# A linear-attention block beside an MLP on one Trainium2 core: another order for loading and transposing x at the start

## The chip, the cores and the metric

The kernel runs on one core of a Trainium2 chip. The metric is device time in microseconds; the time before is 206.69 us, the median of three runs (206.48 to 206.86). The profiles are of one execution each. In them PE is TensorE's matmuls, PEld its weight loads, DVE is VectorE, ACT is ScalarE, POOL is GpSimd and SP is the queue of SyncE, which here issues nearly all DMAs. Times inside a profile are microseconds from the start of its span.

## What is computed

x is 2048 tokens by 640 features in bf16. It is normalized, and the output is x plus a linear attention and plus an MLP of the normalized x, both without any dependence between them:

```python
xn = _layernorm(x, axis=-1)
return x + _A_ref(xn, A_wqkv, A_wo) + _B_ref(xn, B_w1, B_b1, B_w2, B_b2)
```

The part that this document is about is the start: the normalization and the MLP's first layer.

```python
m = jnp.mean(x, axis=axis, keepdims=True)
v = jnp.var(x, axis=axis, keepdims=True)
return (x - m) / jnp.sqrt(v + eps)
...
h = jnp.einsum("bsd,df->bsf", x, w1) + b1
h = _gelu(h)
return jnp.einsum("bsf,fd->bsd", h, w2) + b2
```

W1 is 640 by 1536. The attention has 32 heads of 20 features and needs the projections by Wqkv, for which the same normalized and transposed x is used later.

## The kernel before

Tokens are handled in 16 tiles of 128 (x0 to x15 below), features in five blocks of 128 (k = 0 to 4), the hidden features of the MLP in twelve blocks of 128 (jb = 0 to 11).

**From x to a matmul.** A tile of x is loaded with its tokens on the partitions (dma_x, tile xPK). VectorE takes its statistics in two halves (ln_half, line 357) and joins them (ln_aggr, line 365); GpSimd adds the epsilon (line 360) and raises the variance to the power -1/2 (line 367); VectorE normalizes (ln_norm, line 381, tile xn_tm). For the first layer a tile must then be transposed, features on the partitions (tile xnT). There are two ways. TensorE can transpose five blocks of 128 into PSUM, from where ScalarE or VectorE copies them (tr_part and cp_part for tiles 0 and 1, lines 342, 350 and 351; transp and xnT_copy for tile 2, lines 389 and 397). Or a DMA transposes it from SBUF to SBUF (xnT_dma, line 263, issued by SP), as for tiles 3 to 15.

**The order of matmuls** is the list named plan, written by hand. Tiles 0 and 1 are worked block row by block row of W1 as these rows are loaded (hk, line 439: a token group, a number of tiles, jb, and the blocks k), with all twelve jb open in PSUM banks 0 to 5 at once. Line 439 takes 128 columns where one tile is worked, 256 where both are. Then come the units that have all five k at once: h_pack, line 423, one tile of 128 columns, four jb in one bank; h_unit, line 408, two or four tiles, 256 or 512 columns, one jb. After the last product ScalarE applies the activation and writes HG (lines 446, 428 and 412). Marks in the plan place other work: "T1" the transposes of tile 1 with the statistics of tiles 2 and 3, "TC" the last blocks of tile 0, "T2" the transpose of tile 2 and the normalization of tile 3 and, through ln_rest, all of tiles 4 to 15.

**What sets the order.** Each engine executes its instructions in the order in which the program calls for them, and each instruction waits for what it reads and for the buffers that it writes. So does SP: a DMA transpose that waits for a normalization holds back every DMA behind it. All loads and transposes of this start are issued by SP, except half of x0 and b1. Before, SP issues the loads of x0 to x11 and of W1's five row blocks first (lines 273 to 286), then the transposes of tiles 3 to 7, then the load of x12 to x15, then the transposes of tiles 8 to 15, and then the loads of Wqkv and of the later weights. PSUM banks of the units are taken in turn from a ring of eight (take); at(b) sets the ring to a bank.

The block after this start uses xnT with Wqkv (lines 564 and 570), then the attention's sums, then the output, with the MLP's second layer (line 771).

Of the kernel before, what the change touches and what calls it, by code (L numbers as in the profile page):

```python
# [112 lines left out]
def bass_parallel_sum__linear_attn_block__dense_activation_gelu__prompt_kernel(  # L113
# [27 lines left out]
    with contextlib.ExitStack() as es:  # L141
# [67 lines left out]
        def bank(b, lo=0, hi=512):  # L209
            return ps[:, b * 512 + lo: b * 512 + hi]  # L210
# [58 lines left out]
        def dma_w1(k):  # L269
            dma("sync", W1[:, k, :], w1v[:, k, :], [r_W1[k]])  # L270
# [3 lines left out]
            dma(("sync", s_)[i], x_in[:, 0, lo:hi], xv[0:P, lo:hi], [r_x[0][i]])  # L274
        dma_x(1, 1)
        dma_w1(0)
        dma_w1(1)
        dma_w1(2)
        dma_x(2, 1)
        dma_w1(3)  # L280
        dma_x(3, 1)
        dma_w1(4)
        dma_x(4, 2)
        dma_x(6, 2)
        dma_x(8, 2)
        dma_x(10, 2)

        Pl.ins(v, lambda e: e.memset(pm[0:P // 2], 1.0), writes=[r_pm])
        Pl.ins(v, lambda e: e.memset(pm[P // 2:P], -1.0), writes=[r_pm])
# [93 lines left out]
                    ALU.subtract, ALU.mult),  # L383
                    reads=r_x[t] + [r_aggr[s], r_rstd[t]], writes=[r])

        def transp(t):
            b = take(1)
            pT = bank(b).bitcast(BF16)[:, 0:D]
            Pl.ins(pe, [(lambda e, k=k: e.transpose(pT[:, k * P:(k + 1) * P],
                                                    xn_tm[:, t, k * P:(k + 1) * P], ident[:]))  # L390
                        for k in range(DT)],
                   reads=r_xn[t] + [r_ident], writes=[B_[b]])
            return b

        def xnT_copy(t, b):
            pT = bank(b).bitcast(BF16)[:, 0:D]
            Pl.ins(v, lambda e: e.tensor_copy(xnT[:, :, t * P:(t + 1) * P],
                                              pT.rearrange("p (k q) -> p k q", k=DT)),
                   reads=[B_[b]], writes=r_xnT[t])

        def xnT_dma(t):
            dma_t("sync", xnT[:, :, t * P:(t + 1) * P], xn_tm[:, t, :], r_xnT[t], reads=r_xn[t])

# [28 lines left out]
        def at(b):  # L432
            ring[0] = b
# [43 lines left out]
        k_list = lambda t, n, ks, lo=0, hi=JT: [(t, n, jb, ks) for jb in range(lo, hi)]  # L477
        pack = lambda t, lo, hi: [(t, jb) for jb in range(lo, hi, 4)]
        plan = k_list(0, 1, [0]) + ["T1"] + k_list(0, 1, [1]) + k_list(1, 1, [0]) + k_list(1, 1, [1]) + ["TC"]
        plan += k_list(0, 1, [2]) + k_list(1, 1, [2]) + k_list(0, 2, [3], 0, 8) + ["T2"]  # L480
        plan += k_list(0, 2, [4], 0, 8) + k_list(0, 2, [3, 4], 8)
        plan += pack(2, 0, 8) + h_list(2, 2, 8, JT) + pack(3, 0, 8) + h_list(4, 2, 0, 7) + h_list(6, 2, 0, 7)
        plan += h_list(4, 4, 7, JT) + h_list(8, 4, 0, JT) + h_list(12, 4, 0, JT)

        def ln_rest():
            def out(t):
                ln_norm(t)
                xnT_dma(t)
            ln_stats(5)
            out(4)  # L490
            ln_stats(6)
            out(5)
            ln_stats(7)
            out(6)
            out(7)
            dma_x(12, 4)
            ln_stats(8)
            for t in range(8, NT):
                if t + 1 < NT:
                    ln_stats(t + 1)  # L500
                out(t)

        for u in plan:
            if u == "TC":
                tr_part(0, 2)
                cp_part(0, 2)
            elif u == "T1":
                for i in range(2):
                    tr_part(1, i)
                    cp_part(1, i)  # L510
                ln_stats(2)
                ln_half(3, 0)
                ln_half(3, 1)
                ln_norm(2)
                ln_aggr(3)
            elif u == "T2":
                at(7)
                b = transp(2)
                ln_norm(3)
                xnT_dma(3)  # L520
                xnT_copy(2, b)
                ln_stats(4)
                ln_rest()
            elif len(u) == 2:
                h_pack(*u)
            elif len(u) == 4:
                hk(*u)
            else:
                h_unit(*u)
# [364 lines left out]
```

## Time and profile before

| | us |
|---|---|
| median of three runs | 206.69 |
| lowest and highest | 206.48, 206.86 |
| profiled execution | 206.2 |
| its span | 204.5 |
| TensorE busy | 201.2 |
| VectorE busy | 107.6 |
| ScalarE busy | 70.6 |
| GpSimd busy | 34.1 |

The profiled execution's own time is 1.7 us over its span, and 0.5 us under the median. The granted clock of TensorE was full throughout. The first 13 us are dense in loads, at 303 GB/s in the stretch from 5 to 16 us. The order of DMA issues on SP in this start (start, length of the issue, what):

```profile
1.73 1.37 SPq L260 DMA_DIRECT2D W<-in_B_w_dram  x3
3.14 0.43 SPq L260 DMA_DIRECT2D xPK<-in_A_x_dram  x1
3.62 0.61 SPq L260 DMA_DIRECT2D W<-in_B_w_dram  x1
4.27 0.43 SPq L260 DMA_DIRECT2D xPK<-in_A_x_dram  x1
4.75 0.43 SPq L260 DMA_DIRECT2D W<-in_B_w_dram  x1
5.22 2.84 SPq L260 DMA_DIRECT2D xPK<-in_A_x_dram  x4
12.63 9.09 SPq L263 DMA_TRANSPOSE xnT<-xn_tm  x5
21.77 0.58 SPq L260 DMA_DIRECT2D xPK<-in_A_x_dram  x1
```

The four loads at 5.22 are x4 to x11, in pairs. The five transposes at 12.63 are those of tiles 3 to 7, each waiting for its normalization, and the load at 21.77 is x12 to x15.

### The profile page before, as it was taken

The page shows a single profiled execution, that of the slowest core. Times are in us where ns is not written, and L with a number is a line of the kernel's source. Part 1 is how long each engine was busy: PE and PEld are TensorE (multiplying, and loading weights), DVE is VectorE, ACT ScalarE, POOL GpSimd, SP SyncE. Part 2 cuts the span into 40 slices and gives each one's busy share as a digit, 9 for nine tenths or more (in the row PEclk, how much of TensorE's full clock was granted, in tenths as well). Part 3 has the DMA queues.
Part 4 walks back from the last instruction along what each step waited for, and adds up shares of the span by engine and source line. Part 5 has one row for each costly group of instructions (what it writes and reads, how often), then busy time and mean ns, then how long its engine had stood idle before and what let it go on. Part 6 is the DMA issues. An engine that isn't in the chain of part 4 may idle for free.

```text
span 204.5 us, 3338 instructions
## 1 busy us (share of the span) xinstructions
PE 201.2 (98%) x1230; PEld 104.0 (51%) x1230; DVE 107.6 (53%) x237; ACT 70.6 (35%) x138; POOL 34.1 (17%) x85
## 2 busy tenths in 40 slices
PE   8999999999999999999999999999999999999995
PEld 3899864444444444444546444544444444444443
DVE  3588764000007889499658888534624823513231
ACT  2369976666676555121163554500000000000000
POOL 3235637400000001898000200000000000000000
PEclk9999999999999999999999999999999999999999
DMA  5997678899700111100010000238985622102301
GB/s 161 368 277 93 136 162 99 233 332 363 250 6 0 26 26 26 29 0 0 0 32 5 0 0 16 92 51 197 321 206 127 152 54 55 51 26 51 79 29 51
DMA packets 34457, 21.37 MB, mean 105 GB/s; under 512 B 21384, under 2 KB 33800, under 8 KB 34440
## 3 DMA queue, kind: packets, MB, share of 16 engines
q1 hardware_dynamic: 30384, 17.54, 32.7%
q10 hardware_dynamic: 4056, 3.61, 6.4%
q8 instruction: 10, 0.16, 0.3%
q14 instruction: 7, 0.06, 0.1%
HBM read 13.08 MB, written 2.62 MB: 77 GB/s over the span
## 4 chain that ended last, share of the span: by engine, by line
PE 96%; DVE 1%; DMA 1%; issue 0%; DVEq 0%
PE ps L771 29%; PE ps L408 20%; PE ps L650 11%; PE ps L564 8%; PE ps L597 8%; PE ps L782 7%; PE ps L439 3%; PE ps L423 2%; PE ps L606 2%; PE ps L570 2%; DMA xPK<-in_A_x_dram 1%; DVE stats L357 1%; PE ps L704 1%; PE ps L660 1%; PE ps L714 1%; PE ps L342 0%
## 5 line engine op out<-in xcount | busy, mean ns | idle before, releaser
L771 PE MATMUL ps<-W,HG 128*128 128x512 bf16 (+2 forms) x204 | 43.9, 367 | 0.0
L408 PE MATMUL ps<-xnT,W 128*128 128x512 bf16 (+1 forms) x235 | 41.5, 338 | 0.0
L412 ACT ACTIVATE HG<-ps,b1c 128x512 bf16<-128x512 f32 (+1 forms) x47 | 27.9, 651 | 12.1 <-PE ps L408 11.6
L408 PEld LDWEIGHTS ps<-xnT,W 128*128 128x128 bf16 x235 | 22.8, 98 | 18.0
L771 PEld LDWEIGHTS ps<-W,HG 128*128 128x128 bf16 x204 | 19.4, 98 | 22.2 <-ACT Msb L686 0.2
L552 ACT ACTIVATE ek<-ps 128x512 bf16<-128x512 f32 x40 | 23.8, 597 | 19.4 <-PE ps L650 10.1
L553 DVE TENSOR_SCALAR ek<-ek 128x512 bf16<-128x512 bf16 x40 | 11.5, 287 | 31.4 <-ACT ek L552 31.4
L795 DVE TENSOR_TENSOR W<-ps,xnT 128x512 bf16<-128x512 f32 x15 | 10.4, 691 | 25.1 <-PE ps L771 19.4
L650 PE MATMUL ps<-xnT,Wqkv 128*128 128x512 bf16 x100 | 21.9, 379 | 0.0
L771 PE MATMUL ps<-Msb,PQ 128*128 128x512 bf16 (+2 forms) x85 | 19.6, 367 | 0.0
L564 PE MATMUL ps<-Wqkv,xnT 128*128 128x512 bf16 x80 | 17.9, 379 | 0.0
L591 POOL COPY Wqkv<-Wqkv 128x128 bf16<-128x128 bf16 x25 | 13.9, 558 | 22.4 <-PE ps L570 20.9
L597 PE MATMUL ps<-xPK,xn_tm 128*128 128x512 bf16 x80 | 17.4, 379 | 0.0
L357 DVE BATCH_NORM_STATS2 stats<-xPK 128x6 f32<-128x320 bf16 (+2 forms) x32 | 13.9, 478 | 5.7 <-DMA xPK<-in_A_x_dram 5.7
L650 PEld LDWEIGHTS ps<-xnT,Wqkv 128*128 128x128 bf16 x100 | 9.7, 98 | 11.5
L555 DVE SCALAR_TENSOR_TENSOR PQ<-ps,ek 128x512 bf16<-128x512 f32 x20 | 13.8, 692 | 2.5 <-PE ps L632 0.5
L771 PEld LDWEIGHTS ps<-Msb,PQ 128*128 128x128 bf16 x85 | 8.2, 98 | 9.2
L597 PEld LDWEIGHTS ps<-xPK,xn_tm 128*128 128x128 bf16 x80 | 7.8, 98 | 9.4
L564 PEld LDWEIGHTS ps<-Wqkv,xnT 128*128 128x128 bf16 x80 | 7.8, 98 | 9.4
L555 DVE SCALAR_TENSOR_TENSOR xPK<-ps,ek 128x512 bf16<-128x512 f32 x16 | 11.1, 692 | 1.7
L620 DVE TENSOR_TENSOR Msb<-Msb,xPK 128x640 f32<-128x640 f32 x14 | 11.6, 826 | 0.5
L367 POOL TENSOR_TENSOR rstd<-aggr,mhalf 128x1 f32<-128x1 f32 x16 | 10.0, 623 | 7.4 <-DVE aggr L365 7.4
(79 smaller groups left out, 151.1 us busy)
## 6 DMA issues: line engine op xcount, KB each, us to landing
Wqkv<-in_A_wqkv_dram SPq DMA_DIRECT2D x3, 800.0 KB, 7.4
xnT<-in_A_x_dram SPq DMA_DIRECT2D x4, 512.0 KB, 6.9
W<-in_B_w_dram SPq DMA_DIRECT2D x5, 384.0 KB, 5.2
W<-in_B_w_dram SPq DMA_DIRECT2D x1, 1920.0 KB, 13.1
out_dram<-W ACTq DMA_DIRECT2D x15, 128.0 KB, 1.8
xn_tm<-rden ACTq DMA_DIRECT2D x12, 128.0 KB, 4.6
xPK<-in_A_x_dram SPq DMA_DIRECT2D x4, 320.0 KB, 7.1
Wo<-in_A_wo_dram SPq DMA_DIRECT2D x8, 160.0 KB, 8.7
```

The lines of the kernel that those rows point to most:

```text
L357: Pl.ins(v, lambda e: e.bn_stats(stats[:, s, 6 * h:6 * h + 6], x_in[:, t, lo:hi]), reads=[r_x[t][min(h, len(r_x[t]) - 1)]], writes=[r_stat ...
L408: Pl.ins(pe, [(lambda e, k=k: e.matmul(bank(b, 0, w), W1[:, k, jb * P:(jb + 1) * P], xnT[:, k, tok], start=(k == 0), stop=(k == DT - 1))) ...
L412: Pl.ins(s_, lambda e: e.activation(HG[:, jb, tok], bank(b, 0, w), ACT.Gelu_apprx_tanh, bias=b1c[:, jb:jb + 1]), reads=[B_[b], r_b1c], wri ...
L552: Pl.ins(s_, lambda e: e.activation(e2, src, ACT.Exp), reads=br, writes=[r_ek[s]])
L555: Pl.ins(v, lambda e: e.scalar_tensor_tensor(out=d2, in0=src, scalar=0.0, in1=e2, op0=ALU.max, op1=ALU.add), reads=br + [r_ek[s]], writes= ...
L564: Pl.ins(pe, [(lambda e, k=k, b=b, t=t: e.matmul(bank(b), xnT[:, k, t * P:(t + 1) * P], Wqkv[:, k, D:D + MW], start=(k == 0), stop=(k == D ...
L591: Pl.ins(g, lambda e, k=k, i=i: e.tensor_copy(plain(Wqkv[:, k, D:2 * D], i), parts(Wqkv[:, k, 0:D], i)), reads=[r_Wq], writes=[r_Wk, r_WqP])
L597: Pl.ins(pe, lambda e, t=t, b=b, f=f, i=i: e.matmul(bank(b), xn_tm[:, t, f * P:(f + 1) * P], PK[:, t, 0:MW], start=(i == 0), stop=(i == NT ...
L620: Pl.ins(v, lambda e, t=t: e.tensor_tensor(out=zsum, in0=zsum, in1=PK[:, t, :], op=ALU.add), reads=[r_PK[t], r_PKr[t // CH], r_zsum], writ ...
L650: Pl.ins(pe, [(lambda e, k=k, j=j, b=b: e.matmul(bank(b), Wqkv[:, k, D + j * P:D + (j + 1) * P], xnT[:, k, cc], start=(k == 0), stop=(k == ...
L771: Pl.ins(pe, [(lambda e, i=i, x=x, bk=bk: e.matmul(bank(bk, 0, x[1] - x[0]), seq[i][0], seq[i][1][:, x[0]:x[1]], start=(i == 0), stop=(i = ...
L782: Pl.ins(pe, lambda e, i=i: e.matmul(bank(b), seq[i][0], seq[i][1], start=(i == 0), stop=(i == NS - 1)), reads=seq[i][2], writes=[B_[b]], ...
```

## The change

The loads of x2 and x3 move forward: x2 is issued between W1's row blocks 0 and 1, x3 between 1 and 2. The loads of x4 to x11 leave the head of the program. x4-5 is issued in "T1", which puts it in front of the transpose of tile 3; x6-7 follows that transpose, x8-9 that of tile 4, x10-11 that of tile 5.

The work at the marks changes with it. In "T1", VectorE now normalizes tile 2 and tile 3 and SP issues tile 3's transpose, and the copy of tile 1's second part comes after the first half of tile 3's statistics. "T2", with tile 2's transpose by TensorE into bank 7 and its copy by VectorE, comes eight matmuls of 256 columns later, and between the halves of tile 4's statistics.

In the plan, row block 2 is worked for tiles 0 and 1 together (256 columns). The packs of tiles 2 and 3 cover four jb instead of eight, and the two tiles together the other eight. Tiles 4-5 and 6-7 are worked in pairs for six jb instead of seven, and all four together for six instead of five.

```diff
--- before.py
+++ after.py
@@ -274,16 +274,12 @@
             dma(("sync", s_)[i], x_in[:, 0, lo:hi], xv[0:P, lo:hi], [r_x[0][i]])
         dma_x(1, 1)
         dma_w1(0)
+        dma_x(2, 1)
         dma_w1(1)
+        dma_x(3, 1)
         dma_w1(2)
-        dma_x(2, 1)
         dma_w1(3)
-        dma_x(3, 1)
         dma_w1(4)
-        dma_x(4, 2)
-        dma_x(6, 2)
-        dma_x(8, 2)
-        dma_x(10, 2)
 
         Pl.ins(v, lambda e: e.memset(pm[0:P // 2], 1.0), writes=[r_pm])
         Pl.ins(v, lambda e: e.memset(pm[P // 2:P], -1.0), writes=[r_pm])
@@ -382,21 +378,6 @@
                     xn_tm[:, t, lo:hi], x_in[:, t, lo:hi], aggr[:, s, 0:1], rstd[:, t:t + 1],
                     ALU.subtract, ALU.mult),
                     reads=r_x[t] + [r_aggr[s], r_rstd[t]], writes=[r])
-
-        def transp(t):
-            b = take(1)
-            pT = bank(b).bitcast(BF16)[:, 0:D]
-            Pl.ins(pe, [(lambda e, k=k: e.transpose(pT[:, k * P:(k + 1) * P],
-                                                    xn_tm[:, t, k * P:(k + 1) * P], ident[:]))
-                        for k in range(DT)],
-                   reads=r_xn[t] + [r_ident], writes=[B_[b]])
-            return b
-
-        def xnT_copy(t, b):
-            pT = bank(b).bitcast(BF16)[:, 0:D]
-            Pl.ins(v, lambda e: e.tensor_copy(xnT[:, :, t * P:(t + 1) * P],
-                                              pT.rearrange("p (k q) -> p k q", k=DT)),
-                   reads=[B_[b]], writes=r_xnT[t])
 
         def xnT_dma(t):
             dma_t("sync", xnT[:, :, t * P:(t + 1) * P], xn_tm[:, t, :], r_xnT[t], reads=r_xn[t])
@@ -477,19 +458,21 @@
         k_list = lambda t, n, ks, lo=0, hi=JT: [(t, n, jb, ks) for jb in range(lo, hi)]
         pack = lambda t, lo, hi: [(t, jb) for jb in range(lo, hi, 4)]
         plan = k_list(0, 1, [0]) + ["T1"] + k_list(0, 1, [1]) + k_list(1, 1, [0]) + k_list(1, 1, [1]) + ["TC"]
-        plan += k_list(0, 1, [2]) + k_list(1, 1, [2]) + k_list(0, 2, [3], 0, 8) + ["T2"]
-        plan += k_list(0, 2, [4], 0, 8) + k_list(0, 2, [3, 4], 8)
-        plan += pack(2, 0, 8) + h_list(2, 2, 8, JT) + pack(3, 0, 8) + h_list(4, 2, 0, 7) + h_list(6, 2, 0, 7)
-        plan += h_list(4, 4, 7, JT) + h_list(8, 4, 0, JT) + h_list(12, 4, 0, JT)
+        plan += k_list(0, 2, [2]) + k_list(0, 2, [3], 0, 8) + k_list(0, 2, [4], 0, 8) + ["T2"] + k_list(0, 2, [3, 4], 8)
+        plan += pack(2, 0, 4) + h_list(2, 2, 4, JT) + pack(3, 0, 4) + h_list(4, 2, 0, 6) + h_list(6, 2, 0, 6)
+        plan += h_list(4, 4, 6, JT) + h_list(8, 4, 0, JT) + h_list(12, 4, 0, JT)
 
         def ln_rest():
             def out(t):
                 ln_norm(t)
                 xnT_dma(t)
+            dma_x(6, 2)
             ln_stats(5)
             out(4)
+            dma_x(8, 2)
             ln_stats(6)
             out(5)
+            dma_x(10, 2)
             ln_stats(7)
             out(6)
             out(7)
@@ -500,26 +483,33 @@
                     ln_stats(t + 1)
                 out(t)
 
+        at(6)
         for u in plan:
             if u == "TC":
                 tr_part(0, 2)
                 cp_part(0, 2)
             elif u == "T1":
-                for i in range(2):
-                    tr_part(1, i)
-                    cp_part(1, i)
+                tr_part(1, 0)
+                cp_part(1, 0)
+                tr_part(1, 1)
                 ln_stats(2)
                 ln_half(3, 0)
+                cp_part(1, 1)
+                ln_norm(2)
+                dma_x(4, 2)
                 ln_half(3, 1)
-                ln_norm(2)
                 ln_aggr(3)
-            elif u == "T2":
-                at(7)
-                b = transp(2)
                 ln_norm(3)
                 xnT_dma(3)
-                xnT_copy(2, b)
-                ln_stats(4)
+                t2 = bank(7).bitcast(BF16)[:, 0:D]
+                ln_half(4, 0)
+            elif u == "T2":
+                Pl.ins(pe, [(lambda e, k=k: e.transpose(t2[:, k * P:(k + 1) * P], xn_tm[:, 2, k * P:(k + 1) * P], ident[:]))
+                            for k in range(DT)], reads=r_xn[2] + [r_ident], writes=[B_[7]])
+                Pl.ins(v, lambda e: e.tensor_copy(xnT[:, :, 2 * P:3 * P], t2.rearrange("p (k q) -> p k q", k=DT)),
+                       reads=[B_[7]], writes=r_xnT[2])
+                ln_half(4, 1)
+                ln_aggr(4)
                 ln_rest()
             elif len(u) == 2:
                 h_pack(*u)
```

## The prediction

> **What bounds the kernel now.** I read four views, in this order: the page (busy shares and the chain that ended last), the chain inside the stretch that the change touches, the weight loads of TensorE around two hand-overs, and the DMA issues with their landing times.
>
> The page says that TensorE is never free, and that nearly the whole chain is TensorE:
>
> ```profile
> PE 201.2 (98%) x1230; PEld 104.0 (51%) x1230; DVE 107.6 (53%) x237; ACT 70.6 (35%) x138; POOL 34.1 (17%) x85
> PE 96%; DVE 1%; DMA 1%; issue 0%; DVEq 0%
> ```
>
> So an edit is worth only what it takes from, or adds to, TensorE's own stream. A busy TensorE can still hide short waits, so the stretch is read by count and time. This is the chain from 5 to 35 us (start, length, what), cut to the pieces of the first layer's matmuls:
>
> ```profile
> 6.12 0.83 PE ps L439 x12
> 6.95 0.31 PE ps L342 x5
> 7.26 2.01 PE ps L439 x36
> ...
> 13.63 2.23 PE ps L423 x40
> 15.86 2.32 PE ps L408 x20
> 18.18 2.23 PE ps L423 x40
> 20.41 14.76 PE ps L408 x103
> ```
>
> Forty matmuls of 128 columns take 2.23 us, 55.8 ns each. The last line is 70 of 256 columns and 33 of 512; over the whole stage the chain has 70 and 145 in 38.94 us. The difference, 112 of 512 columns in 24.18 us, gives 215.9 ns, and the rest 109.1 ns for 256 columns. At that rate the twenty at 15.86 should take 2.18 us and take 2.32: 0.14 us is a wait. The weight loads (start, length, group) show it:
>
> ```profile
> 7.05 0.32 PEld L439 LDWEIGHTS ps<-xnT,W 128*128 128x128 bf16 x5
> ...
> 15.31 0.38 PEld L423 LDWEIGHTS ps<-xnT,W 128*128 128x128 bf16 x6
> 15.82 0.88 PEld L408 LDWEIGHTS ps<-xnT,W 128*128 128x128 bf16 x9
> ...
> 19.80 0.43 PEld L423 LDWEIGHTS ps<-xnT,W 128*128 128x128 bf16 x7
> 20.20 0.48 PEld L408 LDWEIGHTS ps<-xnT,W 128*128 128x128 bf16 x5
> ```
>
> The groups of line 408 at 15.82 and 20.20 are the first users of xnT tile 3 and of tiles 4 and 5. The transpose of tile 3 is issued at 12.63 and lands 3.1 us later, at 15.7: that is the wait. At 7.05 the second row block of W1 is first used. Now the DMAs (KB each, median us from issue to landing), each line from a window around one issue:
>
> ```profile
> W<-in_B_w_dram SPq DMA_DIRECT2D x1, 384.0 KB, 4.5
> ...
> xnT<-xn_tm SPq DMA_TRANSPOSE x1, 2.6
> ...
> xPK<-in_A_x_dram SPq DMA_DIRECT2D x1, 640.0 KB, 5.2
> ...
> xnT<-xn_tm SPq DMA_TRANSPOSE x1, 5.2
> ...
> xnT<-in_A_x_dram SPq DMA_DIRECT2D x1, 512.0 KB, 3.7
> ...
> 27.02 0.89 DVE L357 BATCH_NORM_STATS2 stats<-xPK 128x6 f32<-128x320 bf16 x2 [2.35 <-DMA xPK<-in_A_x_dram]
> ```
>
> They are: W1's row block 1, issued at 2.19, so landed at 6.7; the transpose of tile 5, issued at 16.95 behind nothing, landed at 19.55; the load of x12 to x15, issued at 21.77 after the transpose of tile 7, landed at 27.0; the transpose of tile 8, issued at 22.39 behind that load, landed only at 27.6; and x_again's first reload of x (line 742), issued at 126.09 on a quiet queue. The last line, from VectorE's timeline, shows it standing 2.35 us for x12 to x15. What matters is the pair of transposes: 2.6 us alone, 5.2 us behind a load.
>
> **What the Trainium skill says.** "TensorE: Matmul & The Clock Gate", section "Wait — 56ns, not 53.3ns?", gives every warm matmul about 2.5 ns beyond its columns; the 55.8, 109.1 and 215.9 ns here agree (two 128s are 2.5 ns dearer than one 256). "DMA: Bandwidth & Descriptors", section "Queues, rings and completion order", says that each DMA engine consumes one queue's descriptors in ring order; the 5.2 us of tile 8 against 2.6 agree. The same page, "Anatomy of one DMA — SWDGE (gpsimd) path", fits a DMA as 2.0 us plus bytes over 436 GB/s, for another issuer than SP. Here tile 1's 160 KB took 2.4 us (the fit: 2.4), but the 512 KB reload 3.7 (3.2) and the 640 KB load 5.2 (3.5): a load that starts between other work was up to 1.7 us slower.
>
> **The change part by part.**
>
> *Wider matmuls.* The columns streamed stay the same. Twelve pairs of 128 in row block 2 become twelve of 256, and 80 of 128 in the packs of tiles 2 and 3 become 40 of 256: 52 pairs at 2 x 55.8 - 109.1 = 2.5 ns, 0.13 us. Ten of 256 become five of 512: 0.01 us. Gain 0.14 us. ScalarE does 8 activations of 256 columns instead of 16 of 128 (0.43 for 2 x 0.28 us), off the path.
>
> *Tile 3 earlier.* x2 and x3 move forward, so VectorE reaches tile 3 sooner. x2 should land at about 6.0, x3 at 7.6 (from 8.34 and 10.05, less the W1 blocks passed, 1.2 us each). Then two halves of statistics (0.89), 0.2 of aggregation and 0.45 of normalization for each tile and the copy of tile 1 (0.29), with GpSimd's power (0.57) between, put the end of tile 3's normalization at about 11.0 instead of 12.6. Its transpose lands near 13.7 and is wanted at 14.7. The 0.14 us wait goes. TensorE's transpose of tile 2 moves eight matmuls later, to 12.4; VectorE's copy (0.48) then ends near 13.2, and line 423 wants it at 13.5. That leaves 0.3 us of cover; without it each tenth late is a tenth lost.
>
> *W1 one x tile later.* x2 now stands in front of W1's row block 1. x2 lands 0.47 us after the block before it in the old order, so row block 1 lands at 6.7 + 0.47 = 7.17; TensorE wants it at 7.05. Loss 0.13 us. Bounds: 0 if the transfer hides in the queue's start, 0.5 if the smaller packets break the stream. Everything behind waits on TensorE's single stream. Row block 2 comes at about 8.8 (wanted 9.3), row block 3 at 10.0 (wanted 10.6), row block 4 as before at 11.05 (wanted 11.5): covered.
>
> *x6 to x11 between the transposes.* Before, these three loads were issued from 5.7 on and the queue was empty when the transposes came. Now SP issues transpose 3, x6-7, transpose 4, x8-9, transpose 5, x10-11, transposes 6 and 7, x12-15. A transpose holds SP for 1.2 us and a load for about 0.6. VectorE's path to tile 4 has not become shorter: x4-5 still lands at 11.9, the copy of tile 2 comes later, and tile 4 is normalized at about 15.4 (15.5 before). So transpose 4 is issued at 15.4, x8-9 at 16.6, transpose 5 from 17.2, and in ring order it follows x8-9. How long x8-9 takes there, no row shows. Lower bound 2.75 us (the skill's fit for 320 KB, an estimate); upper 5.2 less 320 KB at the 0.39 MB/us that streaming loads reach (0.84), 4.35 us; from the 512 KB reload 3.2 us. I take 3.6, a little over the middle of the bounds because both trace rows lie above the fit. x8-9 then lands at 20.2, and tile 5, like tile 8 after x12-15, 0.6 us later: 20.8, between 19.95 and 21.6. (Waiting for x6-7, issued at 12.3, VectorE finishes tile 5 by 17.4; with 2.6 us that is 20.0, not the later one.) TensorE wants tiles 4 and 5 at 20.20 - 0.27 + 0.13 = 20.06. Loss 0.75 us, bounds 0 and 1.55. TensorE has no other work queued ahead of that wait.
>
> *Behind it.* Tiles 6 and 7 are wanted 30 matmuls (3.3 us) later, at about 24.1, and should land at 23.1 and 23.7. Tiles 8 to 11 are wanted after 33, where the trace has them by 31.2; Wqkv's loads, issued at 36.1, are wanted at 59. Nothing further is charged.
>
> **Sum.** -0.14 - 0.14 + 0.13 + 0.75 = +0.60 us. On the profiled execution, 206.2 us of which the span is 204.5 and 1.7 lie around it, that is 206.8 with a span of 205.1. That execution stands 0.5 us under the median of 206.69, so for the median I forecast 207.3.
>
> **Rivals.**
> - *The loads slip in between (not slower).* If x8-9 lands within 2.8 us of its issue, as a lone 160 KB load did in 2.4, tile 5 arrives at 20.0 and nothing waits: 206.69 - 0.28 + 0.13 = 206.5. For it: x's rows have just been read, and the fit. Against it: both loads issued into a gap in this trace were slower than the fit. It decides from 2.8 us downward. A gain over 0.4 us would need more than all waits I can find.
> - *W1's row block is the loss.* If x2 costs its upper bound, 0.5 us, and tile 5 is in time: 206.9. The trace's even landings (1.1 to 1.2 us a block) speak against it.
> - *A second slip.* x6-7, x8-9 and x10-11 all as slow as x12-15: tile 5 at 21.6, and tile 7 up to 0.3 us behind the later demand: 206.69 - 0.28 + 0.13 + 1.55 + 0.3 = 208.4. For it: VectorE's 2.35 us stand; against it: x12-15 is twice as large.
> - That tile 3 isn't earlier after all would need x3 to land after 9; only the stated order of one queue stands behind it, and I give it nothing of its own.
>
> **Chances.** The forecast 0.52, the loads slipping in 0.33, W1's row block 0.05, a second slip 0.10. A measurement of this kernel can tell about 0.2% (0.41 us) from no change. The forecast's own range is 206.9 to 207.9, nearly all above 207.1. Of the loads slipping in I count 0.08 as a gain beyond 0.2%, for waits that I haven't seen, and the rest as no change; W1's row block is mostly no change. That gives faster 0.08, within 0.2% 0.30, slower 0.62. The range takes in the no-stall end and the second slip: 206.3 to 208.4.
>
> **What would show it.** Right: no wait at the first 256-column group of tile 2 and 3; a gap of about 0.1 us after the five transposes at 6.8; a gap of 0.3 to 1.5 us before the first group on tiles 4 and 5, released by transpose 5; transpose 5 landing over 3 us after its issue. Wrong: tile 5 landing before 20.1, or a gap elsewhere, such as at the pack of tile 2 (the copy from PSUM late) or before tiles 6 and 7.

## The result, and the profile after

The changed kernel takes 208.73 us (median of 6 runs, 207.87 to 209.3), the kernel before, run beside it, 206.68. The ratio is 1.0095, with a 95% interval of 1.0066 to 1.0125: slower, by 2.05 us at the medians, where 0.6 was forecast. The profiled execution of after took 207.87 us with a span of 206.1; before's took 206.2 with 204.5. The pair of traces therefore has to explain 1.7 us. (Of the experiments below, one profiled execution, that of experiment 3's first run, was disturbed, and nothing is read from it.)

TensorE is as busy as before, 201.5 us against 201.2, and the span has grown. The page of after:

```profile
PE 201.5 (98%) x1193; PEld 103.1 (50%) x1193; DVE 107.9 (52%) x237; ACT 70.6 (34%) x133; POOL 34.1 (17%) x85
```

TensorE has 37 matmuls less than the 1230 before. The chain of waits of after from 5 to 40 us, cut to the start of the first layer (start, length, what):

```profile
7.34 2.18 PE ps L420 x36
...
13.85 1.12 PE ps L404 x20
14.96 4.37 PE ps L389 x40
19.33 1.12 PE ps L404 x20
20.45 0.69 issue
21.14 3.44 PE ps L389 x30
24.58 0.65 issue
25.23 14.87 PE ps L389 x83
```

Line 420 is hk (before: 439), 404 the pack (423), 389 the unit with all five k (408). Before, this stretch was PE from piece to piece; now it has two pieces called "issue", where TensorE does nothing. The first lies before the units on tiles 4 and 5, the second before those on tiles 6 and 7. Forty matmuls of 256 columns at 14.96 take 4.37 us, 109 ns each, so the small wait for tile 3 is gone. The weight loads of after give the idle time in the brackets, with what ended it (at 21.11 the profile names nothing, but tile 5's landing, below, comes just before):

```profile
7.34 2.01 PEld L420 LDWEIGHTS ps<-xnT,W 128*128 128x128 bf16 x36 [0.23 <-DMA W<-in_B_w_dram]
...
21.11 3.18 PEld L389 LDWEIGHTS ps<-xnT,W 128*128 128x128 bf16 x30 [0.84 <-issue]
25.20 1.87 PEld L389 LDWEIGHTS ps<-xnT,W 128*128 128x128 bf16 x18 [0.91 <-DMA xnT<-xn_tm]
```

Three waits of 0.23, 0.84 and 0.91 us make 1.98. Less the 0.23 us of the gains (wider matmuls and tile 3, worked out below) that is 1.75. Everything behind is only shifted: in the chain, the first piece after the first layer starts at 59.35 before and 61.04 after, and the last step (W, on VectorE) at 202.21 and 203.90, both times 1.69 us later. The 0.06 us between the two figures lie in the brackets, which are not exactly what is lost: from 21.11 to 25.20 there are 4.09 us, thirty matmuls of 109.1 ns take 3.27 of them, and the loss there is 0.82.

Each wait has a landing behind it. The DMAs of after, each line from a window around one issue (KB each, median us from issue to landing), in the order of SP's queue: the load of x8-9, issued at 16.91; the transposes of tile 5, at 17.82; the load of x10-11, at 19.08; the transposes of tiles 6 and 7, at 19.70 and 20.95.

```profile
xPK<-in_A_x_dram SPq DMA_DIRECT2D x1, 320.0 KB, 3.4
...
xnT<-xn_tm SPq DMA_TRANSPOSE x1, 3.2
...
xPK<-in_A_x_dram SPq DMA_DIRECT2D x1, 320.0 KB, 3.3
...
xnT<-xn_tm SPq DMA_TRANSPOSE x1, 4.8
...
xnT<-xn_tm SPq DMA_TRANSPOSE x1, 4.2
```

Tile 5 lands at 21.05 behind x8-9 (20.27), and TensorE goes on at 21.11. Tiles 6 and 7 land at 24.51 and 25.14, and it goes on at 25.20. But x10-11 had already landed at 22.36; tile 6 needs 2.15 us more, where tile 5 needed 0.78 behind its load. What holds it shows in the DMA view of after from 22 to 26 us (busy share and GB/s in 40 slices of 0.1 us, then one queue's packets, MB and share):

```profile
DMA  8999999999900000000000951990200902162689
GB/s 164 238 216 377 228 189 225 202 146 92 26 0 0 0 0 15 8 10 10 10 10 13 218 134 26 64 77 13 13 0 0 51 13 38 38 77 77 230 320 307
...
q8 instruction: 1, 0.02, 1.9%
```

At 22.30 one packet of 16 KB of queue q8 began, which the profile calls "instruction" (a fetch of instructions, below: the fetch). It took 1.21 us, until 23.51; that is the 1.9% of 16 engines' 4 us in the last line. From 23.1 to 23.5 us no other packet begins, and from there to 24.2 the packets come at about 10 GB/s. Earlier, from 22.4 to 22.8, it was 189 to 228 GB/s, a sixteenth of which is 12 to 14. So the reading is that the fetch held one of the 16 engines, and that the transposes' packets queued on it came out last, one after another, while the other fifteen were done. (The profile doesn't name the engine of a packet.) Such a fetch was there before too, at 19.47, on the same transpose:

```profile
q8 instruction: 1, 0.02, 74.4%
issues: line engine op xcount, KB each, median us to landing
xnT<-xn_tm SPq DMA_TRANSPOSE x1, 3.9
```

(The DMA view of before around 19.45 us.) Tile 6 took 3.9 us instead of 2.6 there, landed at 22.29, tile 7 at 23.19, and TensorE did not come for them until 23.9: hidden.

### The profile page after: what moved, and what is told of

The parts are those of the page before. It is cut to its first block, busy times and chain, and to the rows that moved or that the text cites. A ratio compares the mean times of both kernels' runs of the same rounds, so it can differ in the third digit from the quotient of the medians.

```text
span 206.1 us, 3255 instructions
## 1 busy us (share of the span) xinstructions
PE 201.5 (98%) x1193; PEld 103.1 (50%) x1193; DVE 107.9 (52%) x237; ACT 70.6 (34%) x133; POOL 34.1 (17%) x85
## 4 chain that ended last, share of the span: by engine, by line
PE 95%; DMA 2%; issue 1%; SPq 1%; DVE 0%
PE ps L761 29%; PE ps L389 21%; PE ps L640 10%; PE ps L587 8%; PE ps L554 8%; PE ps L772 7%; PE ps L420 3%; DMA W<-in_B_w_dram 2%; PE ps L596 2%; PE ps L560 2%; PE ps L404 1%; SPq L260 1%; PE ps L694 1%; PE ps L650 1%; PE ps L704 1%
## 5 line engine op out<-in xcount | busy, mean ns | idle before, releaser
L389 PE MATMUL ps<-xnT,W 128*128 128x512 bf16 (+1 forms) x250 | 43.8, 336 | 1.3 <-issue 1.3
L389 PEld LDWEIGHTS ps<-xnT,W 128*128 128x128 bf16 x250 | 24.3, 98 | 20.3 <-DMA xnT<-xn_tm 0.9
L393 ACT ACTIVATE HG<-ps,b1c 128x512 bf16<-128x512 f32 (+1 forms) x50 | 29.5, 626 | 13.8 <-PE ps L389 13.1
L581 POOL COPY Wqkv<-Wqkv 128x128 bf16<-128x128 bf16 x25 | 14.0, 559 | 22.4 <-PE ps L560 20.9
L587 PE MATMUL ps<-xPK,xn_tm 128*128 128x512 bf16 x80 | 17.4, 379 | 0.0
## 6 DMA issues: line engine op xcount, KB each, us to landing
W<-in_B_w_dram SPq DMA_DIRECT2D x1, 1920.0 KB, 13.2
```

The lines of the kernel that those rows point to most:

```text
L389: Pl.ins(pe, [(lambda e, k=k: e.matmul(bank(b, 0, w), W1[:, k, jb * P:(jb + 1) * P], xnT[:, k, tok], start=(k == 0), stop=(k == DT - 1))) ...
L393: Pl.ins(s_, lambda e: e.activation(HG[:, jb, tok], bank(b, 0, w), ACT.Gelu_apprx_tanh, bias=b1c[:, jb:jb + 1]), reads=[B_[b], r_b1c], wri ...
L581: Pl.ins(g, lambda e, k=k, i=i: e.tensor_copy(plain(Wqkv[:, k, D:2 * D], i), parts(Wqkv[:, k, 0:D], i)), reads=[r_Wq], writes=[r_Wk, r_WqP])
L587: Pl.ins(pe, lambda e, t=t, b=b, f=f, i=i: e.matmul(bank(b), xn_tm[:, t, f * P:(f + 1) * P], PK[:, t, 0:MW], start=(i == 0), stop=(i == NT ...
```

## The experiments

Each kernel was run beside the kernel before; ratios are to it, with 95% intervals. Waits are the idle times of the weight loads in the profiled execution, as above; the normal start of W1's row block 0 has about 0.15 us there.

**1. The changed kernel itself, again.**

> The changed kernel itself, for a second trace and more times. Three waits stood in its first trace: 0.27 us before W1's row block 1, 0.90 before tiles 4 and 5, 0.90 before tiles 6 and 7, in an execution of 207.87 us, while the median of its runs was 208.73. Theory S (loads between the transposes hold the transposes behind them back in SP's queue): the same three places, with different lengths; a slower execution has longer waits at tiles 4-5 and 6-7 and nowhere else. Theory W (W1's row block 1 behind x2 is the loss): the wait there varies and explains the spread. Time 207.9 to 209.3.

208.59 us, 1.0117 [1.0082, 1.0153]. (The expectation gives the waits of the first trace with up to 0.06 us of difference from the brackets above.) Its profiled execution, 208.63 us, is nearer to the median than the first one:

```profile
21.32 3.18 PEld L389 LDWEIGHTS ps<-xnT,W 128*128 128x128 bf16 x30 [0.93 <-issue]
25.95 1.11 PEld L389 LDWEIGHTS ps<-xnT,W 128*128 128x128 bf16 x11 [1.45 <-DMA xnT<-xn_tm]
```

With 0.34 for W1 and 0.11 more than usual at row block 0, that is 2.8 us of waits, less 0.23: 2.6 for a span that is 2.4 longer than before's. The wait before tiles 6 and 7 varies most, 0.91 and 1.45: tile 6 took 5.7 us here, with a fetch at 23.47.

**2. After, with all loads of x ahead of the transposes.**

```diff
                 dma_x(4, 2)
+                dma_x(6, 2)
+                dma_x(8, 2)
+                dma_x(10, 2)
                 ln_half(3, 1)
...
-            dma_x(6, 2)
...
-            dma_x(8, 2)
...
-            dma_x(10, 2)
```

> The changed kernel with the loads of x6 to x11 issued right behind x4-5, ahead of transpose 3; all else as changed. Theory S: the waits before tiles 4-5 and 6-7 go; W1's wait of 0.27 stays; transpose 3 again stands behind loads and may cost 0.1 to 0.3 us: 206.6 to 207.0 us. Theory W: no better than 208. Theory F (transposes 6 and 7 are held up by the program's own instruction fetches on the DMA engines, which the trace shows at that time in both kernels): the wait before tiles 6-7 stays at about 0.9, so 207.5.

207.49 us, 1.0051 [1.0033, 1.0069]. Both late waits are gone, and another has come (the weight loads of this kernel):

```profile
15.82 4.26 PEld L389 LDWEIGHTS ps<-xnT,W 128*128 128x128 bf16 x40 [0.87 <-DMA xnT<-xn_tm]
20.09 1.21 PEld L404 LDWEIGHTS ps<-xnT,W 128*128 128x128 bf16 x20
21.26 5.83 PEld L389 LDWEIGHTS ps<-xnT,W 128*128 128x128 bf16 x54
```

The transposes of tiles 5 and 6 land 2.6 us after their issue. The second fetch, at 22.48 here, comes when tile 6 has landed (21.22) and tile 7 (22.53) nearly has. But tile 3's transpose, issued at 10.96, now stands behind 960 KB more of loads, with a fetch at 13.2, and lands at 15.78; so the time was higher than expected. Taking the loads out of the way of transposes 5 to 7 takes the two late waits away, and puts them in the way of another transpose.

**3. Before, with only the loads of x6 to x11 moved between the transposes.**

```diff
         dma_x(4, 2)
-        dma_x(6, 2)
-        dma_x(8, 2)
-        dma_x(10, 2)
...
+            dma_x(6, 2)
             ln_stats(5)
             out(4)
+            dma_x(8, 2)
             ln_stats(6)
             out(5)
+            dma_x(10, 2)
```

> The kernel before with only the loads of x6 to x11 moved between the transposes, W1 and x2, x3 in the old order and the old plan of matmuls. Theory S: tile 5 lands near 21.3 where it is wanted at 20.2, tiles 6 and 7 near 25: 207.8 to 208.8 us, most of the whole loss by this part alone. Theory W: 206.7. Theory F: 206.7 to 207.2.

209.53 us, 1.0144 [1.0119, 1.0169]: more than was expected, and more than the whole change. The same kernel a second time, for its trace:

> The kernel before with only the loads of x6 to x11 moved between the transposes of tiles 3 to 6, a second time, for a trace that can be read. If the loads in front of the transposes make the loss whatever the order at the head: waits of about 0.9 us before tiles 4 and 5 and 0.7 to 1.5 us before tiles 6 and 7, none at W1's row block 1, and a time 1.0 to 2.9 us above before. If the loss needs the new head as well: those two waits together under 0.6 us and less than 0.6 us lost.

210.48 us, 1.0189 [1.0169, 1.0209]. Neither expectation describes it. There is a single wait, and it is long (weight loads; then the busy times by window, where the columns are length, busy us and count of PE, PEld, DVE, ACT and POOL, the granted clock, DMA share and GB/s):

```profile
23.09 5.93 PEld L405 LDWEIGHTS ps<-xnT,W 128*128 128x128 bf16 x43 [2.96 <-issue]
```

```profile
20.40:23.00 2.60, 0.00 (x0) 0.00 (x0) 2.16 (x6) 1.82 (x8) 1.07 (x4) 0.90 1.02 69
23.10:25.70 2.60, 2.58 (x13) 1.81 (x14) 1.50 (x5) 0.73 (x2) 0.92 (x3) 0.50 1.29 200
26.10:28.70 2.60, 2.60 (x26) 2.34 (x24) 1.34 (x5) 2.13 (x5) 1.32 (x3) 1.00 0.70 234
```

x6-7, issued at 13.79, lands at 17.26; VectorE stands 1.98 us for it and finishes tile 5 late, the transpose is issued at 18.82 instead of 16.95, and the fetch at 19.85 falls on it: it lands at 23.03. Then TensorE works at half its clock from 23.09 to about 25.9: 13 matmuls of 256 columns in a window where later 26 fit. That costs about 1.4 us on top of the wait. The Trainium skill ("TensorE: Matmul & The Clock Gate", "What's actually happening") says that an idle stretch makes the clock fall to half; it puts the window at about 3.4 us, and here less was enough: the mean of 0.90 in the first window means that about 0.5 us of it was at half clock, so the clock fell some 2.3 us after the wait began at 20.13. All five executions of this run had a mean clock of 0.991 to 0.992; in the first run one of five had it, and that one took 210.58 us where the others took 208.88 to 209.55. So the loads alone cost about 3 to 4 us in the old order, and the rest of the change takes 1 to 2 of them back.

**4. After, with x2 and x3 one W1 row block later.**

```diff
         dma_w1(0)
-        dma_x(2, 1)
         dma_w1(1)
-        dma_x(3, 1)
+        dma_x(2, 1)
         dma_w1(2)
+        dma_x(3, 1)
```

> The changed kernel with x2 behind W1's row block 1 and x3 behind row block 2. Theory S: the wait of 0.27 before row block 1 goes, but little of it is kept, because TensorE then stands longer before tile 5, whose landing is set by x6-7 and x8-9: 208.3 to 208.7, 0 to 0.3 under the changed kernel. Theory W: back to 206.7 or below.

208.83 us, 1.0102 [1.0083, 1.0121]. The wait for W1's row block 1 is gone, and nothing is gained: 0.27 us have come back before tiles 2 and 3, and those before tiles 4-5 and 6-7 are 0.83 and 1.88. TensorE came earlier to the same landings.

**5. After, with each of the two loads one transpose or more later.**

```diff
             out(4)
-            dma_x(8, 2)
             ln_stats(6)
             out(5)
-            dma_x(10, 2)
+            dma_x(8, 2)
             ln_stats(7)
             out(6)
             out(7)
+            dma_x(10, 2)
             dma_x(12, 4)
```

> The changed kernel with x8-9 issued behind transpose 5 instead of ahead of it, and x10-11 behind transpose 7. Theory S (ring order): transpose 5, with no load directly ahead of it, lands 2.6 us after its issue (3.2 and 3.6 in the two traces of the changed kernel); it is issued at 17.7 because VectorE waits for x6-7, so tile 5 comes at 20.4 and its wait falls from 0.90 to about 0.2. Transpose 6 then follows x8-9 and lands near 23.4 without an instruction fetch, up to 24.7 with one, so the second wait stays, 0 to 1.3. Theory F (it is the instruction fetch alone that makes a transpose late): the wait before tile 5 doesn't change. Time 207.5 to 208.6.

208.37 us, 1.0091 [1.0059, 1.0123]. The weight loads of this kernel:

```profile
20.57 3.18 PEld L389 LDWEIGHTS ps<-xnT,W 128*128 128x128 bf16 x30 [0.15 <-issue]
25.43 1.66 PEld L389 LDWEIGHTS ps<-xnT,W 128*128 128x128 bf16 x16 [1.68 <-DMA xnT<-xn_tm]
```

The transpose of tile 5 (from a window around its issue at 17.94):

```profile
xnT<-xn_tm SPq DMA_TRANSPOSE x1, 2.6
```

With x8-9 behind it, it takes 2.6 us again, and the wait before tiles 4 and 5 falls from 0.84 to 0.15. The 0.15 is left because the transpose itself is issued a microsecond later than before (16.95 there): x6-7 lands at 16.38, and VectorE needs it first. Tile 6's is now the one behind that load (5.0 us, with a fetch at 22.6 in it), and the time goes there.

**6. After, with the load of x8-9 reading rows that have been read already.** The third argument is new: the tile whose rows are read.

```diff
-            dma_x(8, 2)
+            dma_x(8, 2, 4)
```

> The changed kernel with the load at the place of x8-9 reading the rows of x4 and x5 once more, so tiles 8 and 9 are computed from those rows. If the slow start of such a load (about 1 us below the full rate after its first packet) is that of rows not touched before, it goes: the load lands 2.3 to 2.6 us after its issue instead of 3.4, and tile 5 near 20.4. If it belongs to every load that starts after a pause in reading, it stays at 3.3 to 3.5 and the time at 208.0 to 209.

208.75 us, 1.0098 [1.0079, 1.0118]. That load took 3.3 us from its issue (3.4 in after) and the waits stayed at 0.95 and 1.14. Its slowness doesn't come from rows that nobody has read yet.

**7. After, with x6 to x11 loaded through ScalarE's queue.** The third argument is new here too: the issuing engine, s_ for ScalarE.

```diff
                 cp_part(0, 2)
+                for t0 in (6, 8, 10):
+                    dma_x(t0, 2, s_)
...
-            dma_x(6, 2)
...
-            dma_x(8, 2)
...
-            dma_x(10, 2)
```

> The changed kernel with x6 to x11 issued from ScalarE's queue right after its last copy of tile 0 (about 9.5 us), so that no transpose of SP stands behind them in a ring. Theory S: the waits before tiles 4-5 and 6-7 go, transpose 3 lands near 14.2 to 15.0 though the loads run beside it, W1's wait of about 0.3 stays: 206.7 to 207.0 us. If the loads instead slow the transposes as much from another queue, tile 3 lands after 15.5 and the time is 207.3 or more.

208.59 us, 1.0104 [1.0071, 1.0137]: a miss. Tiles 4 to 7 wait for nothing, but the three loads, issued from 9.64 on, share the engines with tile 3's transpose, which takes 5.8 us:

```profile
16.75 3.28 PEld L389 LDWEIGHTS ps<-xnT,W 128*128 128x128 bf16 x31 [1.92 <-DMA xnT<-xn_tm]
```

"DMA: Bandwidth & Descriptors" of the Trainium skill, "Issuing engines are not separate DMA queues", says that DMAs of all issuers run on the same 16 engines and interleave. This trace agrees: a second queue took the loads out of SP's order and not out of the way.

**8. After, with the old packs and groups from tile 2 on.**

```diff
-        plan += pack(2, 0, 4) + h_list(2, 2, 4, JT) + pack(3, 0, 4) + h_list(4, 2, 0, 6) + h_list(6, 2, 0, 6)
-        plan += h_list(4, 4, 6, JT) + h_list(8, 4, 0, JT) + h_list(12, 4, 0, JT)
+        plan += pack(2, 0, 8) + h_list(2, 2, 8, JT) + pack(3, 0, 8) + h_list(4, 2, 0, 7) + h_list(6, 2, 0, 7)
+        plan += h_list(4, 4, 7, JT) + h_list(8, 4, 0, JT) + h_list(12, 4, 0, JT)
```

> The changed kernel with the old plan from the packs on (eight jb in the packs of tiles 2 and 3, seven in the pairs): 40 matmuls of 256 columns become 80 of 128, so TensorE has 80 more instructions before tiles 4-5. The 16 KB instruction fetches come about every 250 records of TensorE. Theory F (a fetch holds one DMA engine for about 1.2 us and with it the transpose in flight): the second fetch moves from 22.3-23.5 to about 19 to 20.5, away from transpose 6: the wait before tiles 6-7 falls from 0.9-1.5 to 0-0.3 and transpose 6 lands under 3.8 us after its issue, while tile 5 may be hit instead and wait up to 2. Theory S alone: fetches play no part; the waits stay 0.9 and, as tiles 6-7 are wanted 0.5 later, 0.4 to 1.0.

208.54 us, 1.0087 [1.0066, 1.0108]. The fetch didn't come earlier: it stands at 23.70. Tile 6 was nearly through by then and landed 0.7 us after x10-11 (24.17 and 23.46), as tile 5 does behind its load in after (0.78); tile 7, issued at 21.77, had the fetch on it and took 4.6 us. In this execution the whole first part ran late (1.04 us at W1's row block 0), so its total says little.

**9. After, with 30 small matmuls ahead of tiles 4 and 5.** Their result is not used; the computation is otherwise whole.

```diff
-        plan += pack(2, 0, 4) + h_list(2, 2, 4, JT) + pack(3, 0, 4) + h_list(4, 2, 0, 6) + h_list(6, 2, 0, 6)
+        plan += pack(2, 0, 4) + h_list(2, 2, 4, JT) + pack(3, 0, 4) + ["F"] + h_list(4, 2, 0, 6) + h_list(6, 2, 0, 6)
...
-            if u == "TC":
+            if u == "F":
+                b = take(1)
+                Pl.ins(pe, [lambda e, b=b: e.matmul(
+                    bank(b)[0:32, 0:32], nc.const_aps.tensor(1.0, [P, 32], BF16), onesm[:, 0:32], start=True, stop=True)
+                    for _ in range(30)], reads=[r_ones], writes=[B_[b]])
+                at(b)
+            elif u == "TC":
```

> The changed kernel with 30 matmuls of 32 columns more, whose result nobody reads, between the pack of tile 3 and the first group on tiles 4-5, where TensorE stands for 0.9 to 1.0 us. If the 16 KB fetch at 22.3 to 23.5 is of TensorE's own instructions, 60 records more bring it forward to 21.1 or before, transpose 6 lands less than 4 us after its issue instead of 4.8 to 5.7, and the wait before tiles 6-7 falls by 0.5 or more: 207.6 to 208.3, less if the 30 take longer than the wait. If the fetch is another engine's, it stays at 22.3 to 23.5 and the time at 208.5 or a little above.

209.06 us, 1.0115 [1.0099, 1.013]. The second fetch stayed with the rest of the program, at 23.42, in a trace that is 0.7 us late from the start; the third one came forward, from 46 to 38 us. So the idea that TensorE's count of instructions sets the second fetch isn't supported, and whose instructions it brings stays open.

**10. After, with the three loads directly behind tile 3's transpose.**

```diff
                 xnT_dma(3)
+                dma_x(6, 2)
+                dma_x(8, 2)
+                dma_x(10, 2)
                 t2 = bank(7).bitcast(BF16)[:, 0:D]
...
-            dma_x(6, 2)
...
-            dma_x(8, 2)
...
-            dma_x(10, 2)
```

> The changed kernel with all three loads of x6 to x11 directly behind transpose 3, one start instead of three. Transpose 3 stays early (no wait before tiles 2-3). x6-7 lands near 16.2 as before, x11 near 18; transpose 4 lands near 19.2, transpose 5 near 20.4 with nothing ahead of it (wait 0.1 to 0.3), transpose 6 near 22 without a fetch and near 23.5 with one, wanted at 23.6 to 23.8. Theory S: 206.8 to 207.4 us, with W1's wait of 0.3 the largest. If a load of any kind between transposes is what costs, whatever stands behind it: 208 or more.

207.63 us, 1.0056 [1.0038, 1.0074], a little above what was expected. No load is directly in front of transposes 5 to 7, and there is still a wait before tiles 6 and 7:

```profile
20.90 3.18 PEld L389 LDWEIGHTS ps<-xnT,W 128*128 128x128 bf16 x30
24.80 2.20 PEld L389 LDWEIGHTS ps<-xnT,W 128*128 128x128 bf16 x21 [0.71 <-issue]
```

Tile 6 took 2.6 us and landed at 22.24; tile 7, issued at 20.91, took 3.8 with the fetch at 22.01 on it. So a fetch on the last transpose of a pair can make this wait without a load directly ahead.

**11. Before, with only x2 and x3 moved forward.**

```diff
         dma_w1(0)
+        dma_x(2, 1)
         dma_w1(1)
+        dma_x(3, 1)
         dma_w1(2)
-        dma_x(2, 1)
         dma_w1(3)
-        dma_x(3, 1)
```

> The kernel before with only x2 and x3 loaded between W1's row blocks, as in the change. The wait before W1's row block 1 comes, 0.27 to 0.45 us as in the traces of the changed kernel; transpose 3 is issued about a microsecond earlier, but behind the loads of x4 to x11, and lands at 15.0 to 15.8 where it is wanted at 15.9: the old wait of 0.14 goes. 206.7 to 207.1 us. Theory W (x2 ahead of W1 is the main loss): 208 or more.

206.97 us against 206.55, 1.0022 [1.0008, 1.0036]: this part costs some 0.4 us. Its profiled execution is one of the faster ones (206.53) and had no wait at W1's row block 1, so the trace doesn't show where. Against the expectation the wait for tile 3 stayed: it is 0.18 us there (0.14 before), behind the same loads of x4 to x11.

**12. After, with the load of x10-11 alone moved behind the transposes.**

```diff
-            dma_x(10, 2)
             ln_stats(7)
             out(6)
             out(7)
+            dma_x(10, 2)
             dma_x(12, 4)
```

> After with the load of x10-11 alone moved from before the transpose of tile 6 to behind that of tile 7. The load of x8-9 stays in front of tile 5's transpose, so the wait before tiles 4 and 5 should stay near 0.9 us. Theory L (the third load makes the wait before tiles 6 and 7, the instruction fetch only adds where it falls on a late transpose): tile 6 lands within about 3 us of its issue and the wait before tiles 6 and 7 is 0 to 0.3 us; median 207.7 to 208.1. Theory F (the instruction fetch makes that wait whatever stands in front): tile 6 or tile 7 still takes 3.8 us or more from its issue, the wait is 0.6 us or more, and the median stays at 208.4 to 208.8.

207.61 us, 1.0052 [1.0036, 1.0069], 1.1 us below after at the medians. One wait is left:

```profile
19.15 1.21 PEld L404 LDWEIGHTS ps<-xnT,W 128*128 128x128 bf16 x20
21.39 7.54 PEld L389 LDWEIGHTS ps<-xnT,W 128*128 128x128 bf16 x66 [1.03 <-issue]
```

The transposes of tiles 6 and 7, in windows around their issues at 18.88 and 20.20:

```profile
xnT<-xn_tm SPq DMA_TRANSPOSE x1, 3.1
...
xnT<-xn_tm SPq DMA_TRANSPOSE x1, 2.6
```

They land at 22.03 and 22.84, the fetch comes at 22.56 and delays neither, and all matmuls from 21.39 on run through. In after's order those transposes were still queued behind x10-11 when the fetch came. So the load in front was needed for that wait.

**13. After, with both loads behind the transpose of tile 7.**

```diff
-            dma_x(8, 2)
             ln_stats(6)
             out(5)
-            dma_x(10, 2)
             ln_stats(7)
             out(6)
             out(7)
+            dma_x(8, 2)
+            dma_x(10, 2)
             dma_x(12, 4)
```

> After with the loads of x8-9 and of x10-11 both behind the transpose of tile 7; x6-7 stays between the transposes of tiles 3 and 4. If the loads in front of transposes 5 and 6 are the whole of the two late waits: tiles 5 and 6 land within 2.8 us of their issue unless the instruction fetch falls on them, the wait before tiles 4 and 5 is under 0.3 us as with x8-9 behind transpose 5, the wait before tiles 6 and 7 is under 0.8 us, and the median is 206.8 to 207.4. If something else in the new order is worth most of the loss: the median stays above 207.6, where the version with the third load alone moved stands.

208.96 us, 1.0107 [1.0088, 1.0126]: no better than after. Tiles 4 and 5 don't wait. But tile 7 is hit by the fetch at 21.76 (4.2 us), and a new wait has opened far behind:

```profile
24.88 9.01 PEld L389 LDWEIGHTS ps<-xnT,W 128*128 128x128 bf16 x58 [0.89 <-issue]
...
36.11 2.93 PEld L389 LDWEIGHTS ps<-xnT,W 128*128 128x128 bf16 x15 [1.78 <-issue]
```

x8-9 lands only at 26.36, VectorE starts tile 8 there, its transpose is issued at 29.01 (23.85 in after), and the one of tile 11 lands at 35.89, too late for the group of tiles 8 to 11. So behind tile 7's transpose x8-9 comes too late for its own tiles. The expectation reads a median above 207.6 as something else in the new order making most of the loss; that doesn't follow, because this edit makes a wait of its own.

**14 and 15. Two versions that were to beat both kernels.** Both start from before, work row block 2 for tiles 0 and 1 together, and move one load, x10-11: in the first behind tile 3's transpose, in the second behind tile 7's.

```diff
-        dma_x(10, 2)
...
-        plan += k_list(0, 1, [2]) + k_list(1, 1, [2]) + k_list(0, 2, [3], 0, 8) + ["T2"]
+        plan += k_list(0, 2, [2]) + k_list(0, 2, [3], 0, 8) + ["T2"]
...
                 xnT_dma(3)
+                dma_x(10, 2)
```

> The kernel before with x10-11 alone behind transpose 3 (the loads of x4 to x9 stay in front) and row block 2 worked for both tiles at once: what is left of the change where the waits allow it. Transpose 3 lands near 15.3 instead of 15.8 and its wait of 0.14 us goes, 0.03 from the wider matmuls, nothing behind: 206.4 to 206.6 us, hardly to be told from before. If x10-11 holds transpose 4 or 5 back past 20.1, it is slower than before.

> The kernel before with row block 2 worked for tiles 0 and 1 together and only the load of x10-11 moved, here behind the transpose of tile 7 instead of behind that of tile 3. The version behind transpose 3 kept a wait of 0.39 us before tiles 6 and 7, from the instruction fetch on transpose 7. If a load queued ahead of transposes 4 to 7 still costs a little: 205.8 to 206.1, below that version. If the fetch alone sets that wait: the same as that version, 206.1 to 206.4.

The first takes 206.18 us (13 runs), 0.9984 [0.9975, 0.9992]; the second 206.24 (21 runs), 0.9985 [0.9976, 0.9994]. Both are faster than before by about 0.3 us, and they can't be told apart: a cost of the place behind tile 3 over the one behind tile 7 doesn't show. In the chain of the second there is no idle piece over 0.05 us from 6 us to the end of the first layer:

```profile
13.61 2.23 PE ps L422 x40
15.84 2.18 PE ps L407 x20
18.03 2.23 PE ps L422 x40
20.26 7.64 PE ps L407 x70
```

The twenty matmuls at 15.84 take 2.18 us where they took 2.32, so the wait for tile 3 is gone: its transpose was issued at 12.42, with a load less ahead of it, and landed at 15.08. Of the 0.3 us this is 0.14, and the twelve wider matmuls of row block 2 are 0.03 (12 times 2.5 ns); the rest is open. The fetch at 20.80 fell on tile 7, which took 4.2 us and landed at 23.64, still in time. In the first version's profile it took 4.7, and TensorE waited 0.35 us for it.

## Why the prediction was wrong

The direction was right, and so was the mechanism at tiles 4 and 5; about half of the loss came from a place that the forecast put at nothing. Term by term, on the profiled pair (in brackets the second profile of after):

| step | forecast | measured |
|---|---|---|
| wider matmuls and tile 3 earlier | -0.28 | -0.23: the 0.14 at tile 3 is gone; 0.09 worked out for the matmuls |
| W1's row block 1 | +0.13 | 0.23 (0.34 in the second profile) |
| tile 5 behind x8-9 | +0.75 | 0.84 (0.93) |
| tiles 6 and 7, "nothing further is charged" | 0 | 0.91 (1.45) |
| sum | +0.60 | +1.75 (+2.6, with 0.11 at row block 0) |
| shift of all that follows | | +1.69 (+2.4, the span) |

*Wider matmuls.* The forecast counted 80 of 128 columns that become 40. The plan before has 80 in the packs of tiles 2 and 3, and half of them stay: 40 become 20. With row block 2 that is 32 pairs and not 52, 0.08 us instead of 0.13, and 0.01 for the five of 512. The pages agree: 1230 matmuls before and 1193 after, 37 less, which is 32 and 5.

*What held.* x8-9 was put at 3.6 us from issue and took 3.36; tile 5 at 20.8, landed at 21.05; TensorE wanted it at 20.06 by the forecast and came at 21.11 less 0.84, 20.27. The ring order behind this is shown by moving the load behind the transpose (2.6 us again, experiment 5). One thing in it was off: the transpose was issued at 17.82, where the forecast had VectorE done by 17.4. The rival that the loads slip in between is refuted by the same landings.

*The step that failed* is "Behind it": tiles 6 and 7 "should land at 23.1 and 23.7" and are wanted at about 24.1. "Nothing further is charged" for them, and the wait there is 0.91 us: tiles 6 and 7 were wanted at 24.29, and landed at 24.51 and 25.14. A gap before tiles 6 and 7 was among the forecast's own signs of being wrong. The loads alone would have given about what was forecast: x10-11 landed at 22.36, and 0.7 us behind a load, as with tile 5 and in experiment 8, makes 23.1. What was missed is the instruction fetch, which the DMA view shows between the two. In before it lay on tile 6's transpose, with 3.9 us against 2.6 for tile 5 in the same profile, and with 0.7 us of margin. The forecast took 2.6 us as a transpose's time, from the one line that it showed, and didn't ask why tile 6 took 1.3 more. With x10-11 ahead, the transposes of tiles 6 and 7 move into a place where such a delay is waited for. The two causes can't be added: without the load there the fetch comes too late to matter (experiment 12); without the fetch the load should leave some half a microsecond of margin (tile 7 at about 23.7), which is argued and not shown, because in every trace of after and its variants with that load in place a fetch fell on tile 6 or 7.

*The rival that came nearest* was the second slip at 208.4: it has the late load and charges tile 7 with 0.3 us. It named the place and not the cause. That its number is close to the measured 208.73 is luck: it has tile 5 at 21.6 and 1.55 us lost there, where 21.05 and 0.84 were measured.

*W1's row block 1* was a little dearer than said and is worth less than said: without its wait (experiment 4) the time stays the same, since TensorE then waits longer at tiles 2 to 7. In before's order, where hardly anything waits later, the early x2 and x3 cost 0.4 us. A wait ahead of later waits for fixed landings can't be added to them.

*The median* lies 0.86 us above after's profiled execution. The second profile, close to the median, has the same waits, longer. The runs of the changed kernel spread over 1.4 us in the first set; how they differ was read in two traces only. One execution of the second set, 210.79 us, had a mean clock of 0.992, as the executions of experiment 3 with a half-speed stretch; it has no trace.

*Open:* whose instructions the fetch near 22 us brings; why loads issued between transposes start slowly; where the 0.4 us of experiment 11 go, and where about half of the 0.3 us of experiments 14 and 15 comes from.

## What to carry to other kernels

A load in a queue of DMA transposes is paid by the transpose behind it and by whoever waits for that one; what is left of the queue then meets events, like an instruction fetch, that had been hidden before. So before an order is tightened, read each transfer's own landing and not the group's typical one, and ask what made the slow ones slow. Where one engine is the bound, a wait ahead of other waits is not worth its length: follow the landings that it will come to next.

## What the runs showed of the hardware

- A fetch of instructions through q8 is one packet of 16 KB. The one near 20 to 25 us took 0.94 to 1.59 us in the traces read here, and the rate while the transposes drain is that of one DMA engine of 16. The transpose that it fell on took 3.8 to 4.7 us with no load directly ahead of it (before, experiments 10, 11, 13, 14, 15), against 2.6.
- A 320 KB load issued between two transposes took 3.1 to 4.0 us in after and its variants; one whose rows had been read already took 3.3.
- In the trace with a wait of 2.96 us TensorE's clock fell to half some 2.3 us into the wait, and the first 2.8 us of work behind it ran at half speed, at a cost of about 1.4 us. Waits up to 1.92 us in the profiled executions had no such stretch.
